# Attention and a low-rank mixer with its two layers on one core: batch 0 mixed by channel blocks, early layer products, w1's first half loaded ahead of batch 1, and batch 1's pairs moved into the later batches' loop

## The chip, the cores and the metric

The kernel runs on one core of one Trainium2 chip. The metric is the device time of one execution in microseconds (us); the median of three runs before the change is 366.27 us (366.23 to 368.55).

## The reference

There are 8 batches, 8 heads, 576 tokens of 64 channels, and 16 "beacon" keys and values ahead of each head's own. The attention is causal, except that all queries see the beacons. Its output, heads side by side, is x (576 tokens by 512 channels); a low-rank mix over tokens and a two-layer network follow.

```python
scores = scale * np.matmul(q, k_all.transpose(0, 1, 3, 2))      # k_all: beacon_k, then k
scores = np.where(causal, -1000000000.0, scores)
a = np.exp(scores - scores.max(-1, keepdims=True))
a /= a.sum(-1, keepdims=True) + 1e-09
x = np.matmul(a, v_all)                                         # heads put side by side
xt = x.transpose(0, 2, 1)
h = xt @ U @ V                                                  # U: 576 x 32, V: 32 x 576
u = x + h.transpose(0, 2, 1)
ch = np.maximum(u @ w_ch1, 0.0) @ w_ch2                         # 512 -> 2048 -> 512
return u + ch
```

## The kernel before

The order of every engine's instructions is the order in which the program writes them. Five engines work side by side: PE (TensorE, matrix products), DVE (VectorE), ACT (ScalarE), POOL (GpSimd, which here issues the casting loads and does a few casts) and SP (which issues the loads of batch 0's q and k, the DMA transposes and the stores).

**Pairs.** Two heads are one pair; a batch has four pairs (NH2 = 4), and pairs are counted through the batches: 0 to 3 are batch 0, 4 to 7 batch 1. For each pair there are these units:

- Regrouping (`regroup`, L220): q and k of the pair are copied into token order (`pr`).
- `qkT_units` (L223): five PE transposes each of q and k into PSUM (`tps`, L229, L231), then two DVE copies each into `qT` and `kT` (L232, L233). From pair 12 on DMA transposes and `order_units` (L257) do this instead.
- `score_units` (L267): `sc[0]` has the scores of key groups 0 and 1 (L286) and four exps on ACT (L292), `sc[1]` groups 2 and 3 and four more exps, `sc[2]` the causal masks on DVE (L273, L275). `sc[0](n)` puts n identity matmuls ahead of the scores (`keep_warm`, L211).
- `av_unit` (L306), one per head: 15 products of exps with values (L310), reciprocal and multiply on DVE (L318, L319) into the batch's `xb`.

**Mix.** `mix_units` (L323) of a batch has `head` (L334: U's products for the four blocks of 128 channels, side by side on PE into one PSUM tile, copied to `qts`) and two `part`s (L348: token tiles 0 and 1, then 2 to 4; for each channel block the transpose of `xb`, L354, plus V's product, L364, copied into `uT` by ACT or DVE).

**Layers.** The mixed tokens of all batches stand in `uT`, cut into nine blocks of 512. `mlp_units` (L378) of a block has 16 `g_unit`s (first layer, four products of 512 columns and a relu on ACT or DVE, L397 to L403) and 16 quarter `c_unit`s (second layer, four products each; the last quarter also stores, L413 to L431). They go into `queue`; `fill(n)` issues the next n of them between the attention's units.

**The order.** Batches 0 and 1 (NF = 2) run in a first loop (L644). Its turn for pair p does the second scores of pair p + 1, the masks of p, the regrouping, transposes and copies of p + 2 around the two heads of p, and the first scores of p + 2. `FIRST` says how many units of the queue are spread over a turn: none in batch 0, then 10, 5, 4, 4. After a batch's last pair, `mix(b)` puts its mix into the queue; batch 0's comes out at once, as the queue is empty, and `feed` adds the layer units of the block that is complete. Batches 2 to 7 run in a second loop (L682), whose turn for pair p has another order: 

```python
seq = sc[0:1] + av[0:1] + qk[0:1] + sc[1:3] + qk[1:2] + av[1:2]
```

Here `sc` are the scores of p + 1, `qk` the transposes of p + 2, and regrouping stands ahead of all. `QUOTA` units of the queue go into a turn: 4 in batch 2, 9 after it. Between the loops, `fill(AHEAD)` issues 16 units.

**Loads.** POOL's queue has, in order: v of batch 0 in two halves, k and q of batch 1 in two halves (`HALVES`: heads 0 to 3, 4 to 7), the first half of its v, the two halves of w1 (`emit_w1`), the casts of U and V (`cast_small`), v's second half, w2 in two halves, and the loads of batch 2 (`load_batch`).

**Memory.** All PSUM tiles share eight banks (`pst`); the four exp tiles `expt0` to `expt3` are used by two pairs in turn.

Of the kernel before, what the change touches and what calls it, by code (L numbers as in the profile page):

```python
# [9 lines left out]
F16 = mybir.dt.float16  # L10
F32 = mybir.dt.float32
# [6 lines left out]
P = 128  # L18
# [9 lines left out]
def kernel(  # L28
# [13 lines left out]
    nc = tc.nc  # L42
# [17 lines left out]
    NT = NC  # L60
# [38 lines left out]
    def pst(shape, dtype, name):  # L99
        return psum.tile(shape, dtype, tag="ps", name=name)  # L100
# [61 lines left out]
    def beacon_load(eng, src, dst, hs):  # L162
        eng.dma_start(out=dst[0:Nb], in_=src[hs].rearrange("h p d -> p h d"))  # L163
# [24 lines left out]
    def k_loads(b, L, hs):  # L188
        main_load(nc.gpsimd, k[b], L[1][0][:, hs, :], hs)
        head_load(nc.gpsimd, k[b], L[0][0][:, hs, :], hs, Nb)  # L190
# [29 lines left out]
        copy(out=t, in_=by_token(L[1][i][:, 2 * c : 2 * c + 2, :]))  # L220
        return t

    def qkT_units(L, pr, qT, kT, c):  # L223

        hs = ds(2 * c, 2)

        def one(i, dst, w):
            ps = pst([P, SK], F16, name="tps")
            nc.tensor.transpose(ps[:, 0:NL], L[0][i][:NL, hs, :], ident[:NL, :NL])  # L229
            for j in range(4):  # L230
                nc.tensor.transpose(ps[:, ds(NL + P * j, P)], pr[i][:, j, :, :], ident)  # L231
            nc.vector.tensor_copy(out=dst[:, c, 0 : w - 4 * P], in_=ps[:, 0 : w - 4 * P])  # L232
            nc.vector.tensor_copy(  # L233
                out=dst[:, c, w - 4 * P : w].rearrange("x (p j) -> x p j", j=4),
                in_=ps[:, NL:SK].rearrange("x (j p) -> x p j", j=4),
            )

        return [lambda: one(1, qT, S), lambda: one(0, kT, SK)]
# [136 lines left out]

        return turn, head, [lambda: part([0, 1]), lambda: part([2, 3, 4])]

    def mlp_units(t0, n, dst, flip, turned=True):  # L378


        units = []
        gT = {}

        def turn():
            ut = utp.tile([P, 4, DM], F16, name="ut", tag="ut")
            for cc in range(NCC):
                nc.sync.dma_start_transpose(out=ut[:, :, ts(cc, P)], in_=uT[:, cc, ds(t0, 4 * P)])
            gT["u"] = ut

        def g_unit(dc):  # L390
            if dc == 0:
                gT["t"] = gtp.tile([P, NDC, 512], F16, name="gT", tag="gT")
                if turned:
                    turn()
            g = pst([P, 512], F32, name="gps")
            for cc in range(NCC):
                nc.tensor.matmul(  # L397
                    g[:, 0:n], w1[:, cc, ts(dc, P)], uT[:, cc, ds(t0, n)], start=(cc == 0), stop=(cc == NCC - 1)
                )
            if (dc % 3 if not turned else (dc + flip) % 2 or dc in (5, 6, 7)):  # L400
                nc.scalar.activation(out=gT["t"][:, dc, 0:n], in_=g[:, 0:n], func=AF.Relu)  # L401
            else:
                nc.vector.tensor_scalar_max(out=gT["t"][:, dc, 0:n], in0=g[:, 0:n], scalar1=0.0)  # L403

        cps = {}

        def c_unit(i, part):
            m = min(P, n - P * i)
            if part == 0:
                cps["t"] = pst([P, DM], F32, name="cps")  # L410
            ps = cps["t"]
            for dc in range(4 * part, 4 * part + 4):
                nc.tensor.matmul(  # L413
                    ps[:m, :], gT["t"][:, dc, ds(P * i, m)], w2[:, dc, :], start=(dc == 0),
                    stop=turned and dc == NDC - 1, skip_group_check=True,
                )
            if part == 3:
                ob = outp.tile([P, DM], F32, name="ob", tag="ob")
                if not turned:
                    for cc in range(NCC):  # L420
                        nc.tensor.matmul(
                            ps[:m, ts(cc, P)], uT[:, cc, ds(t0 + P * i, m)], ident, start=False, stop=True,
                            skip_group_check=True,
                        )
                if turned:
                    nc.vector.tensor_tensor(out=ob[:m, :], in0=ps[:m, :], in1=gT["u"][:m, i, :], op=ALU.add)  # L426
                elif i % 2:
                    nc.scalar.activation(out=ob[:m, :], in_=ps[:m, :], func=AF.Copy)
                else:
                    nc.vector.tensor_copy(out=ob[:m, :], in_=ps[:m, :])  # L430
                nc.sync.dma_start(out=dst(i, m), in_=ob[:m, :])  # L431

        units += [lambda dc=dc: g_unit(dc) for dc in range(NDC)]
        for i in range((n + P - 1) // P):
            units += [lambda i=i, part=part: c_unit(i, part) for part in range(4)]
        return units
# [29 lines left out]
    def load_batch(b):  # L466
        Ls[b] = qk_tiles()
        emit_loads(b, Ls[b], vss[b % 2])
# [35 lines left out]
    def group_first(c, i, copy):  # L504

        prs.setdefault(c, []).append(regroup(Ls[0], c, i, copy))
        hs = SETS[c]
        copy(out=Ls[0][0][i][:NL, hs, :], in_=raw["head"][:NL, i, hs, :])
# [28 lines left out]
    def qkT_of(p):  # L537
        b, c = divmod(p, NH2)
        new_qT_of(p)
        if p in raw_of:  # L540
            return order_units(raw_of[p], qTs[b], kTs[b % 2], c)
        return qkT_units(Ls[b], prs[p], qTs[b], kTs[b % 2], c)

    def scores_of(p):
        b, c = divmod(p, NH2)
# [9 lines left out]


    NF = 2
    HB = 3
    AHEAD = 16
    LAG = 12  # L560
    HINT = 5

    FIRST = [0, 0, 0, 0, 10, 5, 4, 4]

    QUOTA = {2: 4}

    IDLE = [10, 3, 2, 2]
    queue = []
# [9 lines left out]
    def feed(b):  # L578

        while state["t"] < NBLK and 512 * (state["t"] + 1) <= S * (b + 1):  # L580
            t = state["t"]
            queue.extend(
                mlp_units(512 * t, 512, lambda i, m, t=t: rows[ds(512 * t + P * i, m), :], t % 2, t > 0)
            )
            state["t"] += 1

    def mix(b):

        turned = b >= NF and len(queue) >= LAG + 5
        turn, head, parts = mix_units(xbs[b], S * b, turned)  # L590
        if turned:
            turn()
        n = LAG if turned else 2 if b >= NF else 0
        seq = queue[0:n] + [head] + queue[n : n + 3]
        rest = queue[n + 3 :]
        for u in parts:
            seq += [u] + rest[0:3]
            rest = rest[3:]
        queue[:] = seq + rest
        feed(b)  # L600

    with tc.manual_schedule(engines={ENG.PE, ENG.Activation, ENG.DVE, ENG.SP, ENG.Pool}):
# [25 lines left out]

        Ls[1] = qk_tiles()
        group_first(3, 0, G)  # L630
        k_loads(1, Ls[1], HALVES[0])
        q_loads(1, Ls[1], HALVES[0])
        beacon_load(nc.gpsimd, beacon_k[1], Ls[1][0][0], ALLH)
        k_loads(1, Ls[1], HALVES[1])
        q_loads(1, Ls[1], HALVES[1])
        v_loads(v[1], beacon_v[1], vss[1], HALVES[0])
        emit_w1(0)
        emit_w1(1)
        cast_small()
        v_loads(v[1], beacon_v[1], vss[1], HALVES[1])  # L640
        emit_w2()

        NP1 = NF * NH2
        for p in range(NP1):  # L644
            b, c = divmod(p, NH2)
            if c == 0 and NF <= b + 1:
                load_batch(b + 1)
            seq = [masks]
            if p + 1 < NP1:
                seq.insert(0, sc[1])  # L650
                masks = sc[2]
            av, qk, sc = av_of(p), [], []
            if p + 2 < NP1:
                if p == 0:
                    seq.append(lambda: group_first(2, 1, V))
                elif p > 1:
                    seq.append(lambda p=p: regroup_of(p + 2))
                qk = [lambda i=i, p=p: qkT_of(p + 2)[i]() for i in range(2)]
            seq += av[0:1] + qk + av[1:2]
            if p + 2 < NP1:  # L660
                new_qT_of(p + 2)
                sc = scores_of(p + 2)
                if p == 0:
                    seq.append(lambda: group_first(3, 1, act_copy))
                seq.append(lambda sc=sc, p=p: sc[0](IDLE[3] if p < NH2 else 0))
            done = 0
            for i, u in enumerate(seq):
                u()
                want = FIRST[p] * (i + 1) // len(seq)
                fill(want - done)  # L670
                done = want
            if c == NH2 - 1:
                mix(b)

        fill(AHEAD)
        regroup_of(NP1)
# [140 lines left out]
```

## Time and profile before

| | |
|---|---|
| median of three runs | 366.27 us (366.23 to 368.55) |
| the profiled execution | 367.15 us, span 365.5 us |
| PE busy | 349.8 us, 96% of the span |
| DVE, ACT, POOL busy | 204.7, 173.7 and 83.9 us |
| first layer (L397), second layer (L413) | 576 matmuls each, 135.7 and 134.4 us |
| exps (L292) | 256, 111.1 us, 531 ns each |
| DMA | 40.52 MB, mean 111 GB/s |

The page divides the span into 40 slices of 9.1 us, and each digit is the busy share of an engine in tenths. Matmuls overlap, so the mean of one (379 ns for 512 columns) is longer than the distance from one to the next. A line of the timeline gives start and duration in us, engine, line, operation, tiles and count, and in brackets the idle time ahead of it with what ended it.

### The profile page before, as it was taken

The page shows a single profiled execution, that of the slowest core. Times are in us where ns is not written, and L with a number is a line of the kernel's source. Part 1 is how long each engine was busy: PE and PEld are TensorE (multiplying, and loading weights), DVE is VectorE, ACT ScalarE, POOL GpSimd, SP SyncE. Part 2 cuts the span into 40 slices and gives each one's busy share as a digit, 9 for nine tenths or more (in the row PEclk, how much of TensorE's full clock was granted, in tenths as well). Part 3 has the DMA queues.
Part 4 walks back from the last instruction along what each step waited for, and adds up shares of the span by engine and source line. Part 5 has one row for each costly group of instructions (what it writes and reads, how often), then busy time and mean ns, then how long its engine had stood idle before and what let it go on. Part 6 is the DMA issues. An engine that isn't in the chain of part 4 may idle for free.

```text
span 365.5 us, 7721 instructions
## 1 busy us (share of the span) xinstructions
PE 349.8 (96%) x3040; PEld 173.5 (47%) x3040; DVE 204.7 (56%) x565; ACT 173.7 (48%) x382; POOL 83.9 (23%) x123
## 2 busy tenths in 40 slices
PE   7777999999999999999999999999999999999995
PEld 3544545545545444544445444544454555444442
DVE  4887664357776675565666666756566446223311
ACT  3976660177654553466436643674356503401300
POOL 8976436400336001800081005000000000000000
PEclk9989999999999999999999999999999999999999
DMA  9999999990999952999299917942141013013112
GB/s 178 212 151 184 194 201 156 176 170 10 145 136 163 178 80 59 121 190 137 60 111 206 131 35 101 150 74 41 63 120 26 2 57 103 14 59 87 31 44 79
DMA packets 117916, 40.52 MB, mean 111 GB/s; under 512 B 93680, under 2 KB 112112, under 8 KB 117872
## 3 DMA queue, kind: packets, MB, share of 16 engines
q0 software_dynamic: 65904, 17.54, 54.4%
q1 hardware_dynamic: 51520, 22.12, 31.0%
q8 instruction: 25, 0.41, 0.5%
q10 hardware_dynamic: 448, 0.30, 0.3%
q14 instruction: 19, 0.16, 0.1%
HBM read 37.86 MB, written 9.44 MB: 129 GB/s over the span
## 4 chain that ended last, share of the span: by engine, by line
PE 85%; DMA 6%; DVE 3%; ACT 2%; POOL 2%; issue 0%; DVEq 0%; POOLq 0%
PE cps L413 34%; PE gps L397 33%; PE po L310 6%; PE sps L286 6%; DMA w<-in_moe_w_ch_dram 2%; DMA raw<-pr 2%; PE ups L354 2%; DMA st<-in_q_dram 2%; ACT expt L292 2%; PE idle L211 1%; POOL vs L173 1%; DVE gT L403 1%; PE ups L364 1%; PE qtp L339 1%; PE tps L231 1%; DVE expt L273 1%
## 5 line engine op out<-in xcount | busy, mean ns | idle before, releaser
L292 ACT ACTIVATE expt<-sps 128x496 f16<-128x496 f32 (+2 forms) x256 | 111.1, 531 | 61.9 <-PE sps L286 61.7
L397 PE MATMUL gps<-uT,w 128*128 128x512 f16 x576 | 135.7, 379 | 1.8 <-ACT uT L374 1.2
L413 PE MATMUL cps<-w,gT 128*128 128x512 f16 x576 | 134.4, 379 | 0.0
L401 ACT ACTIVATE gT<-gps 128x512 f16<-128x512 f32 x86 | 51.8, 608 | 64.3 <-PE gps L397 62.0
L413 PEld LDWEIGHTS <-gT 128*128 128x128 f16 x576 | 52.3, 98 | 61.1 <-issue 3.7
L397 PEld LDWEIGHTS <-w 128*128 128x128 f16 x576 | 51.8, 98 | 60.8 <-issue 6.1
L403 DVE TENSOR_SCALAR gT<-gps 128x512 f16<-128x512 f32 x58 | 40.1, 691 | 45.7 <-PE gps L397 44.0
L426 DVE TENSOR_TENSOR ob<-cps,ut 128x512 f32<-128x512 f32 x32 | 22.1, 691 | 49.6 <-PE cps L413 49.1
L173 POOL DMA_DIRECT2D vs<-in_v_dram x50 | 40.8, 831 | 14.3 <-DMA st<-in_q_dram 4.9
L310 PEld LDWEIGHTS <-expt 128*128 128x128 f16 (+1 forms) x960 | 36.9, 98 | 15.0 <-DVE expt L273 2.2
L310 PE MATMUL po<-vs,expt 128*128 128x65 f16 (+1 forms) x960 | 40.3, 195 | 1.0 <-DVE expt L273 0.5
L286 PE MATMUL sps<-qT,kT 64*128 64x80 f16 (+4 forms) x384 | 33.4, 286 | 4.0 <-DVE kT L233 3.4
L319 DVE TENSOR_TENSOR xb<-po,rec 128x320 f16<-128x320 f32 x64 | 31.4, 491 | 2.2
L374 ACT ACTIVATE uT<-ups 128x240 f16<-128x240 f32 (+1 forms) x32 | 11.5, 416 | 39.3 <-PE ups L364 39.2
L273 DVE TENSOR_TENSOR expt<-expt,bigmask 128x512 f16<-128x512 f16 x64 | 26.7, 418 | 6.0 <-ACT expt L292 5.9
L163 POOL DMA_DIRECT2D vs<-in_beacon_v_dram x10 | 5.4, 538 | 100.6 <-PE po L310 100.3
L318 DVE RECIPROCAL rec<-po 128x5 f32<-128x5 f32 x64 | 12.0, 187 | 27.0 <-PE po L310 26.2
L286 PEld LDWEIGHTS <-kT 64*128 64x128 f16 x384 | 12.3, 95 | 30.1 <-issue 10.8
L372 DVE CAST uT<-ups 128x240 f16<-128x240 f32 (+1 forms) x32 | 13.1, 450 | 8.5 <-PE ups L364 8.5
L220 DVE COPY pr<-st 128x512 f16<-128x512 f16 x56 | 14.2, 296 | 1.0 <-DMA st<-in_q_dram 0.6
L260 DVE COPY qT<-raw 128x512 f16<-128x512 f16 x20 | 12.4, 619 | 2.7 <-DMA raw<-pr 2.7
L275 DVE TENSOR_TENSOR expt<-expt,mask 80x80 f16<-80x80 f16 x64 | 12.5, 196 | 0.0
(65 smaller groups left out, 157.2 us busy)
## 6 DMA issues: line engine op xcount, KB each, us to landing
out_dram<-ob SPq DMA_DIRECT2D x36, 256.0 KB, 2.3
w<-in_moe_w_ch_dram POOLq DMA_DIRECT2D x4, 1024.0 KB, 11.5
st<-in_k_dram POOLq DMA_DIRECT2D x6, 512.0 KB, 10.0
st<-in_q_dram POOLq DMA_DIRECT2D x6, 512.0 KB, 13.4
vs<-in_v_dram POOLq DMA_DIRECT2D x18, 128.0 KB, 7.5
stm<-in_k_dram SPq DMA_DIRECT2D x4, 256.0 KB, 4.6
vs<-in_v_dram POOLq DMA_DIRECT2D x12, 64.0 KB, 6.2
stm<-in_q_dram SPq DMA_DIRECT2D x3, 256.0 KB, 5.7
```

The lines of the kernel that those rows point to most:

```text
L173: nc.gpsimd.dma_start(out=dst[a : a + nq[j], j, :, :], in_=src[hs, ds(q0[j], nq[j]), :].rearrange("h p d -> p h d"))
L220: copy(out=t, in_=by_token(L[1][i][:, 2 * c : 2 * c + 2, :]))
L273: nc.vector.tensor_tensor(out=e4, in0=e4, in1=bigmask, op=ALU.min)
L286: nc.tensor.matmul(ps[g, i][:, ds(o, w)], kT[hp, c, ds(P * ch, P)], qT[hp, c, ds(qa, w)], start=True, stop=True,)
L292: nc.scalar.activation(out=ex[i][:, ds(SLOT * g, gw[g])], in_=ps[g, i][:, 0 : gw[g]], func=AF.Exp, scale=scale)
L310: nc.tensor.matmul(po[:, j, :], ex[0 : nk[c], ds(blk[(c, j)], P)], vs[0 : nk[c], ds(c * H * E + h * E, E)], start=(c == 0), stop=(c == j),)
L319: nc.vector.tensor_tensor(out=xb[:, :, ds(h * D, D)], in0=po[:, :, 0:D], in1=r.broadcast_to([P, NT, D]), op=ALU.mult)
L397: nc.tensor.matmul(g[:, 0:n], w1[:, cc, ts(dc, P)], uT[:, cc, ds(t0, n)], start=(cc == 0), stop=(cc == NCC - 1))
L401: nc.scalar.activation(out=gT["t"][:, dc, 0:n], in_=g[:, 0:n], func=AF.Relu)
L403: nc.vector.tensor_scalar_max(out=gT["t"][:, dc, 0:n], in0=g[:, 0:n], scalar1=0.0)
L413: nc.tensor.matmul(ps[:m, :], gT["t"][:, dc, ds(P * i, m)], w2[:, dc, :], start=(dc == 0), stop=turned and dc == NDC - 1, skip_group_check ...
L426: nc.vector.tensor_tensor(out=ob[:m, :], in0=ps[:m, :], in1=gT["u"][:m, i, :], op=ALU.add)
```

## The change

- The k copies of pair 0 are done by ACT instead of DVE (`copies`).
- POOL issues the first half of w1 ahead of k and q of batch 1, the casts of U and V and w1's second half behind the first halves of these.
- Batch 0 has a loop of its own (turns p = 0 to 3). Its mix goes by channel blocks (`mix_blocks`): U's products for blocks 0 and 1 as soon as pairs 0 and 1 are done, then these two blocks, then block 2 around the masks of pair 3, and block 3 after pair 3.
- The first four `g_unit`s of block 0 (`EARLY`) are split: the products of channel blocks 0 to 2 come ahead of batch 1's first transposes, the product of block 3 between the units of pair 4.
- Batch 1's pairs are no longer begun during batch 0. Pair 4's transposes and scores and pair 5's transposes follow the mix, and pairs 4 to 7 run in the second loop's order, each pair's regrouping directly ahead of its transposes, with 3, 2, 2 and 1 units of the queue per turn (`FIRST`).
- `AHEAD` is 8 instead of 16, `QUOTA` in batch 2 is 6 instead of 4, and batch 1's mix starts two units later in the queue.

```diff
-    def qkT_units(L, pr, qT, kT, c):
+    def qkT_units(L, pr, qT, kT, c, copies=(None, None)):
...
+            copy = copies[i] or nc.vector.tensor_copy
...
-            nc.vector.tensor_copy(out=dst[:, c, 0 : w - 4 * P], in_=ps[:, 0 : w - 4 * P])
-            nc.vector.tensor_copy(
+            copy(out=dst[:, c, 0 : w - 4 * P], in_=ps[:, 0 : w - 4 * P])
+            copy(
...
+    def mix_blocks(xb, u0):
+        qts = small.tile([P, P], F16, name="qts", tag="qts")
+
+        def head(ccs):
+            qtp = pst([P, P], F32, name="qtp")
+            for j in range(NT):
+                for cc in ccs:
+                    nc.tensor.matmul(
+                        qtp[ds(R * cc, R), :], Usb[: nq[j], j, :], xb[: nq[j], j, ts(cc, P)],
+                        start=(j == 0), stop=(j == NT - 1), skip_group_check=True,
+                        tile_position=(0, R * cc),
+                    )
+            rs = ds(R * ccs[0], R * len(ccs))
+            nc.vector.tensor_copy(out=qts[rs, :], in_=qtp[rs, :])
+
+        def block(cc, copies):
+            rs = ds(R * cc, R)
+            for js, copy in zip(([0, 1], [2, 3, 4]), copies):
+                a, n = q0[js[0]], sum(nq[j] for j in js)
+                ups = pst([P, n], F32, name="ups")
+                for j in js:
+                    nc.tensor.matmul(
+                        ups[:, ds(q0[j] - a, nq[j])], xb[: nq[j], j, ts(cc, P)], ident[: nq[j], : nq[j]],
+                        start=j == js[0], stop=False, skip_group_check=True,
+                    )
+                nc.tensor.matmul(
+                    ups, qts[rs, :], Vsb[rs, ds(a, n)], start=False, stop=True, skip_group_check=True,
+                )
+                copy(out=uT[:, cc, ds(u0 + a, n)], in_=ups)
...
-    def mlp_units(t0, n, dst, flip, turned=True):
+    def mlp_units(t0, n, dst, flip, turned=True, early=0):
...
-        def g_unit(dc):
+        def g_unit(dc, ccs=range(NCC)):
...
-            for cc in range(NCC):
+            for cc in ccs:
...
+            if ccs[-1] < NCC - 1:
+                return
...
-        units += [lambda dc=dc: g_unit(dc) for dc in range(NDC)]
+        for ccs in (range(NCC - 1), range(NCC - 1, NCC)):
+            units += [lambda dc=dc, ccs=ccs: g_unit(dc, ccs) for dc in range(early)]
+        units += [lambda dc=dc: g_unit(dc) for dc in range(early, NDC)]
...
-        return qkT_units(Ls[b], prs[p], qTs[b], kTs[b % 2], c)
+        return qkT_units(Ls[b], prs[p], qTs[b], kTs[b % 2], c, (act_copy, None) if p == 0 else (None, None))
...
+    NP1 = NF * NH2
...
-    AHEAD = 16
+    AHEAD = 8
...
-    FIRST = [0, 0, 0, 0, 10, 5, 4, 4]
-
-    QUOTA = {2: 4}
+    EARLY = 4
+    FIRST = [3, 2, 2, 1]
+
+    QUOTA = {2: 6}
...
-        n = LAG if turned else 2 if b >= NF else 0
+        n = LAG if turned else 2
...
+        emit_w1(0)
         k_loads(1, Ls[1], HALVES[0])
         q_loads(1, Ls[1], HALVES[0])
         beacon_load(nc.gpsimd, beacon_k[1], Ls[1][0][0], ALLH)
+        cast_small()
+        emit_w1(1)
+        v_loads(v[1], beacon_v[1], vss[1], HALVES[0])
         k_loads(1, Ls[1], HALVES[1])
         q_loads(1, Ls[1], HALVES[1])
-        v_loads(v[1], beacon_v[1], vss[1], HALVES[0])
-        emit_w1(0)
-        emit_w1(1)
-        cast_small()
         v_loads(v[1], beacon_v[1], vss[1], HALVES[1])
         emit_w2()
...
+        for p in range(NH2):
+            if p < NH2 - 1:
+                sc[1]()
+            if p < NH2 - 1:
+                masks()
+            av = av_of(p)
+            if p < 2:
                 masks = sc[2]
+                if p == 0:
+                    group_first(2, 1, V)
+                run(av[0:1] + turned_of(p + 2) + av[1:2], 0)
+                if p == 0:
+                    group_first(3, 1, act_copy)
+                sc = scores_of(p + 2)
+                sc[0](IDLE[3])
+            else:
+                masks = sc[2]
+                run(av, 0)
+            if p == NH2 - 2:
+                head, block = mix_blocks(xbs[0], 0)
+                head([0, 1])
+                for cc, copies in ((0, (act_copy, act_copy)), (1, (act_copy, act_copy))):
+                    block(cc, copies)
+                head([2])
+                masks()
+                block(2, (V, V))
+        feed(0)
+        load_batch(2)
+        fill(EARLY // 2)
+        head([NCC - 1])
+        block(NCC - 1, (V, act_copy))
+        fill(EARLY // 2)
+        regroup_of(4)
+        run(turned_of(4), 1)
+        sc = scores_of(4)
+        run(sc[0:2], 1)
+        regroup_of(5)
+        run(turned_of(5), 1)
+        run(sc[2:3], 2)
+        for p in range(NH2, NP1):
+            sc = scores_of(p + 1) if p + 1 < NP1 else []
+            qk = []
             if p + 2 < NP1:
+                qk = turned_of(p + 2)
+                qk[0] = lambda p=p, u=qk[0]: (regroup_of(p + 2), u())
+            av = av_of(p)
+            seq = sc[0:1] + av[0:1] + qk[0:1] + sc[1:3] + qk[1:2] + av[1:2]
             done = 0
             for i, u in enumerate(seq):
                 u()
-                want = FIRST[p] * (i + 1) // len(seq)
+                want = FIRST[p - NH2] * (i + 1) // len(seq)
                 fill(want - done)
                 done = want
-            if c == NH2 - 1:
-                mix(b)
+        mix(1)
```

(`run(us, n)` issues the units `us` with `fill(n)` behind each; `turned_of(p)` are the two transposing units of pair p. The old body of the first loop, which the new loops replace, is left out of this diff.)

More of the change, by code (lines that the diff above doesn't have):

```diff
@@ L376, in mix_units @@
         return turn, head, [lambda: part([0, 1]), lambda: part([2, 3, 4])]
-    def mlp_units(t0, n, dst, flip, turned=True):
+    def mix_blocks(xb, u0):
[25 more added lines that the diff above has]
+                copy(out=uT[:, cc, ds(u0 + a, n)], in_=ups)
+        return head, block
+    def mlp_units(t0, n, dst, flip, turned=True, early=0):
         units = []
         gT = {}
+        gps = {}
         def turn():
@@ L388, in turn @@
             gT["u"] = ut
-        def g_unit(dc):
-            if dc == 0:
+        def g_unit(dc, ccs=range(NCC)):
+            if dc == 0 and ccs[0] == 0:
                 gT["t"] = gtp.tile([P, NDC, 512], F16, name="gT", tag="gT")
@@ L394, in g_unit @@
                     turn()
-            g = pst([P, 512], F32, name="gps")
-            for cc in range(NCC):
+            if ccs[0] == 0:
+                gps[dc] = pst([P, 512], F32, name="gps")
+            g = gps[dc]
+            for cc in ccs:
                 nc.tensor.matmul(
@@ L582, in feed @@
             queue.extend(
-                mlp_units(512 * t, 512, lambda i, m, t=t: rows[ds(512 * t + P * i, m), :], t % 2, t > 0)
+                mlp_units(
+                    512 * t, 512, lambda i, m, t=t: rows[ds(512 * t + P * i, m), :], t % 2, t > 0, 0 if t else EARLY
+                )
             )
@@ L633 @@
         beacon_load(nc.gpsimd, beacon_k[1], Ls[1][0][0], ALLH)
+        cast_small()
+        emit_w1(1)
+        v_loads(v[1], beacon_v[1], vss[1], HALVES[0])
         k_loads(1, Ls[1], HALVES[1])
         q_loads(1, Ls[1], HALVES[1])
-        v_loads(v[1], beacon_v[1], vss[1], HALVES[0])
-        emit_w1(0)
-        emit_w1(1)
-        cast_small()
         v_loads(v[1], beacon_v[1], vss[1], HALVES[1])
         emit_w2()
[L643 to L650, printed above, removed]
-                masks = sc[2]
-            av, qk, sc = av_of(p), [], []
-            if p + 2 < NP1:
[L654 to L665, printed above, removed]
@@ new lines, in run, with turned_of @@
+        def run(us, n):
+            for u in us:
+                u()
+                fill(n)
+        def turned_of(p):
+            return [lambda i=i: qkT_of(p)[i]() for i in range(2)]
+        for p in range(NH2):
[5 more added lines that the diff above has]
+            if p < 2:
+                masks = sc[2]
+                if p == 0:
[16 more added lines that the diff above has]
+                block(2, (V, V))
```

## The prediction

> **What bounds the kernel now.** I read the busy slices of the page first, then stretches of 5 us, then TensorE's timeline where it is not full.
>
> ```profile
> span 365.5 us, 7721 instructions
> PE   7777999999999999999999999999999999999995
> PEclk9989999999999999999999999999999999999999
> ```
>
> TensorE is full from the fifth slice on; only the first four (36 us) and the last one have room. So whatever the change does, it can win only in the first 36 us, and it loses wherever it makes a new hole behind them.
>
> ```profile
> 20.00:25.00 5.00, 3.27 (x52) 2.11 (x50) 3.94 (x14) 3.22 (x8) 3.54 (x6) 0.85 1.54 164
> 25.00:30.00 5.00, 4.21 (x64) 2.73 (x62) 4.25 (x15) 3.60 (x9) 5.00 (x11) 0.81 1.22 107
> 30.00:35.00 5.00, 3.69 (x72) 2.56 (x69) 3.41 (x13) 4.49 (x12) 2.88 (x5) 1.00 1.12 211
> 35.00:40.00 5.00, 5.00 (x44) 2.79 (x45) 3.52 (x9) 1.19 (x2) 0.90 (x1) 1.00 1.40 195
> ```
>
> The columns are the stretch, its length, then busy us of PE, its weight loads, DVE, ACT and POOL, the granted clock, DMA share and GB/s. From 20 to 35 us PE is busy 11.2 of 15 us and part of that runs at a lower clock; from 35 us on it has no hole. What ends the holes:
>
> ```profile
> 20.47 0.61 PE L310 MATMUL po<-vs,expt 128*128 128x65 f16 x15 [0.17 <-DVE expt L275]
> 22.65 0.21 PE L229 MATMUL tps<-ident,hd 80*128 80x80 f16 x1 [1.56 <-DMA hd<-in_q_dram]
> 26.25 0.92 PE L310 MATMUL po<-vs,expt 128*128 128x65 f16 x15
> 34.93 1.90 PE L397 MATMUL gps<-uT,w 128*128 128x512 f16 x8 [0.58 <-DMA w<-in_moe_w_ch_dram]
> ```
>
> Batch 1's first pair waits 1.56 us for its load, and the first layer product starts at 34.93, when w1's first half lands. (At 26.25 one head's values product takes 0.92 instead of about 0.61: the clock is half there.) The fourth view is the loop into which batch 1's pairs are moved, as batch 2 runs it now:
>
> ```profile
> 82.86 0.58 PE L286 MATMUL sps<-qT,kT 64*128 64x496 f16 x4
> 83.36 1.95 ACT L292 ACTIVATE expt<-sps 128x496 f16<-128x496 f32 x4
> 85.16 0.64 ACT L401 ACTIVATE gT<-gps 128x512 f16<-128x512 f32 x1
> 85.64 1.59 ACT L292 ACTIVATE expt<-sps 128x496 f16<-128x496 f32 x4
> 87.15 0.42 DVE L273 TENSOR_TENSOR expt<-expt,bigmask 128x512 f16<-128x512 f16 x1
> 88.04 0.19 DVE L232 COPY kT<-tps 128x80 f16<-128x80 f16 x1
> 88.15 0.68 DVE L233 COPY kT<-tps 128x512 f16<-128x512 f16 x1
> 88.90 0.58 PE L286 MATMUL sps<-qT,kT 64*128 64x496 f16 x4
> ```
>
> This is a closed ring: scores of a pair, four exps, a relu, four exps, masks, the k copies of the pair after it, its scores. It takes 88.90 - 82.86 = 6.04 us (0.50 to the first exp, 1.80, 0.48, 1.51, 0.89 for masks, 0.86 for k copies and the way to PE), and about 5.6 without the relu. TensorE's work in it is a pair's 2.35 us (transposes 0.54, scores 0.90, two heads at 0.46) and four layer units at 0.865, 5.8 in all, so the ring is hidden with 0.2 us to spare. With fewer units it is not.
>
> **The change, part by part.** *k copies of pair 0 to ACT.* DVE now copies q from 6.57 and k until 8.06, scores start at 8.12. An ACT copy of 512 columns took 0.60 (L374's rows 0.42 for 240 to 336); the two beside DVE's end near 7.6. Pair 1 still waits for its load at 8.56, and ACT then runs 16 exps without a hole; by the mask of pair 0, which waits for ACT, about 0.4 us reaches pair 3 (bounds 0 and 0.5). I take 0.4.
>
> *Warm-ups.* Four of 23 identity matmuls go. They stand in PE's waits: nothing; if the clock falls for it, see the second rival.
>
> *Loads.* POOL issues w1's first half (0.78 us) at about 14.1, where k of batch 1 went. The transfers behind each other on that queue keep their order: in the trace q's first half landed at 22.33 (15.49 + 6.84) and w1's halves came at about 5.3 us each. So w1's first half lands near 24.5, q's first half near 22.3 + 5.3 = 27.6, the second halves of k and q (now near 25.7) behind both halves of w1 and half of v (3.5): 25.7 + 10.6 + 3.5 = 39.8.
>
> ```profile
> 26.16 1.52 POOL L149 DMA_DIRECT2D w<-in_moe_w_ch_dram x2
> 35.17 0.90 POOL L155 DMA_DIRECT2D w<-in_moe_w_ch_dram x1 [2.29 <-DMA w<-in_moe_w_ch_dram]
> 41.81 0.88 POOL L155 DMA_DIRECT2D w<-in_moe_w_ch_dram x1 [5.74 <-issue]
> ```
>
> POOL holds an issue until the one eight before it has landed (w2's halves stand exactly eight behind w1's). By that, k's second half is held until w1's second lands (near 33), behind it v's second half and w2; the queue is still full then, so it costs nothing. The small casts now wait for V (issued by 14.4, 5.7 to land: 20.1) and hold the second half of w1 until 20.8, while 6 us of transfers lie ahead of it: nothing. w2 is done near 52.5, as before, and is wanted near 58.
>
> *Batch 0's mix by blocks.* The same matmuls, but U's products no longer go four side by side: 15 steps for 5 at 0.055, and V's eight one after another (0.10 and 0.14) for two groups of 0.2: about 1.1 us more PE, in a stretch where PE waits for exps and masks anyway.
>
> *From 20 to 32 us*, on three engines: the scores of pair 3 stand at 19.0, its exps end at 22.8 (eight at 0.42). Heads 4 and 5: 20.1 to 21.0. Then reciprocal and multiply (0.62 a head) on DVE, the copy qts at 22.2, blocks 0 and 1 until 23.2, block 2's head, masks until 24.8, heads 6 and 7 24.45 to 25.4, two early products (three quarters of 0.865) until 26.7, a wait of 0.35 for head 7, block 3 until 28.2, two more until 29.5. Batch 1's first pair is transposed there, both w1's half and q having landed; DVE does q copies 0.7, a relu 0.6, k copies 0.7 before its scores can start at 32.05, and PE idles 1.5 of it. By 37.96 pair 4's scores, pair 5's transposes and eight layer units are done. That is 0.54 + 0.90 + 0.54 + 8 x 0.865 = 8.9 us of work; before has by then both pairs' transposes and scores, head 8, half of pair 6's transposes and three units, 6.2: 2.7 us in hand.
>
> *Batch 1 in the ring.* Its units per pair are 3, 2, 2, 1 (FIRST), so PE has 4.95, 4.1 and 3.5 us for a ring of 5.6 to 6.04. In the first two rounds regrouping moved between the reciprocal and the transpose: after a head ends, 0.2 + 0.62 + 0.40 + 0.1 = 1.3 us pass before PE can go on, and the second scores stand behind it (in the fourth view they start 2.2 after the first, here 3.4). Round one: scores at 37.96, exps to 40.5, second scores 41.4, relu, exps to 43.6, masks 44.5, a relu 45.1, k copies 45.85: 7.9 us. Round two: from 45.9, second scores 48.5, exps 50.4, masks 51.3, k 52.05: 6.2. Round three has no k copies, but heads 14 and 15 wait for exps until 55.9 and the mask until 56.4; they end at 57.4, unit 15 at 58.2.
>
> *The sum.* At 58.2 all 16 second-layer units of block 0 are left. Before has 14 left at 58.03, so it stood there at 58.03 - 2 x 0.865 = 56.3. The change is 1.9 late. Six units for four in batch 2 give 7.5 us of PE work for its ring of 6.04, so two of its holes close, 0.18 at 82 and 0.68 at 101 (times between matmul starts above the usual 0.216); the one at 76 (0.57) returns, as regrouping 0.8 stands behind the mix's copies: 0.9 back. The 62 units for 55 by batch 2's end shift work to the tail, which is full PE either way. Together +1.0 us: the profiled execution's 367.15 (span 365.5 and 1.65 around it) becomes 368.15; it lies 0.9 over the median, so on the median's scale 366.27 + 1.0 = **367.3**.
>
> **Rivals.** *Faster: the ring hides.* If second scores, exps and masks overlap as well as a full PE would let them, 37.96 to the end of unit 15 is work alone, 14.4 us (three pairs' scores, eight heads, two pairs' transposes, eight units): 52.4, 3.9 ahead of 56.3; with the 0.9 that is -4.8, 361.5. For it: 2.7 us in hand at 38. Against it: the ring row, which no PE order shortens; half of the gain is likelier (364).
>
> *Slower: the clock falls in batch 1.* The half clock of 23.5 to 26.9 followed a hole of 1.56 us with little else in its 3.4 us. My schedule has 1.2 us of matmuls from 44.0 to 47.4. If the clock then halves for 3.4 us, 2.6 us of work take up to 5.2, less 0.8 of waits: +1 to +2.6. [...] With second halves of k and q 1 to 2 us late (39.8 wanted at 39.8; everything on PE behind them waits) it gives +3 to +5.6: 369.3 to 371.9.
> [...]
>
> *Nothing moves.* The products only trade places and each hole filled opens one of equal size: 366.3.
>
> **How the numbers follow.** Forecast (0 to +2.6 us, its own range 366.3 to 368.9): 0.45; nothing to a gain under 2 us: 0.12; the ring partly or wholly hidden: 0.17; the clock or late loads: 0.26. Range: 363.4 (a half gain and some) to 370.4 (the slower rival's middle). One per cent, 3.7 us, is about what a measurement of this kernel can tell from no change. Over it: the upper half of the hidden ring, 0.11 faster; about half of the slower rival, 0.14 slower; the rest, 0.75, within.
>
> **What would show it.** Right: the first layer product near 25.5, a hole near 31, scores of pairs 5, 6 and 7 starting 6 to 8 us apart with PE idle 1 to 2 us before each, head 15 ending near 57, batch 2 without holes. Wrong: those scores 5 us apart (faster rival), or PEclk below 9 beyond slice four, or transposes of pair 6 waiting for hd or st (slower).

## The result, and the profile after

The changed kernel takes 372.51 us (median of four runs, 371.29 to 374.14); the kernel before, beside it on the same chip, 366.25 us (366.07 to 368.55). The ratio is 1.0161, with a 95% interval of 1.0135 to 1.0187: slower by 1.6%, where 367.3 was forecast and 363.4 to 370.4 allowed. (Here and below a ratio is estimated from the fast executions alone, so it need not equal the ratio of the two medians.) The profiled execution takes 371.29 us, its span is 369.6.

The page of the changed kernel, its first line and the busy slices:

```profile
span 369.6 us, 7703 instructions
PE   7786879999999999999999999999999999999995
PEclk9999899999999999999999999999999999999999
```

The third slice (18 to 28 us) is fuller than it was, but the fourth, fifth and sixth (28 to 55 us) are down to 6, 8 and 7, where they were 7, 9 and 9, and the clock dips in the fifth. The same stretches of 5 us as before the change (stretch, length, busy us of PE, weight loads, DVE, ACT, POOL, then clock, DMA share, GB/s):

```profile
20.00:25.00 5.00, 4.29 (x67) 2.70 (x61) 2.76 (x10) 4.60 (x12) 2.31 (x4) 1.00 1.32 200
25.00:30.00 5.00, 4.67 (x54) 2.63 (x55) 3.95 (x15) 0.10 (x1) 4.20 (x6) 1.00 1.25 208
30.00:35.00 5.00, 3.51 (x30) 1.64 (x29) 2.34 (x7) 1.82 (x4) 1.84 (x3) 1.00 1.58 147
35.00:40.00 5.00, 3.41 (x18) 1.74 (x17) 2.19 (x5) 3.37 (x9) 5.00 (x8) 0.73 1.44 115
```

From 20 to 30 us PE is fuller, as was meant: 8.96 us busy instead of 7.48. From 30 to 40 us it is busy for 6.92 instead of 8.69, and part of that runs at a low clock. TensorE's timeline shows where:

```profile
22.68 0.27 PE L406 MATMUL ups<-Vsb,qts 32*128 32x240 f16 x1 [0.51 <-DVE qts L394]
22.89 0.32 PE L402 MATMUL ups<-ident,xb 128*128 128x128 f16 x3
...
25.85 1.09 PE L311 MATMUL po<-vs,expt 128*128 128x65 f16 x30
26.78 1.46 PE L435 MATMUL gps<-uT,w 128*128 128x512 f16 x6
...
33.72 0.58 PE L287 MATMUL sps<-qT,kT 64*128 64x496 f16 x4 [1.49 <-DVE kT L234]
...
37.28 0.61 PE L232 MATMUL tps<-ident,pr 128*128 128x128 f16 x4 [1.39 <-DVE pr L220]
37.68 1.91 PE L435 MATMUL gps<-uT,w 128*128 128x512 f16 x4
...
42.96 0.58 PE L287 MATMUL sps<-qT,kT 64*128 64x496 f16 x4
...
45.38 0.40 PE L232 MATMUL tps<-ident,pr 128*128 128x128 f16 x4 [1.24 <-DVE pr L220]
...
50.62 0.58 PE L287 MATMUL sps<-qT,kT 64*128 64x496 f16 x4 [1.01 <-DVE kT L234]
...
52.98 0.40 PE L232 MATMUL tps<-ident,pr 128*128 128x128 f16 x4 [1.18 <-DVE pr L220]
...
56.65 0.58 PE L287 MATMUL sps<-qT,kT 64*128 64x496 f16 x4 [0.31 <-DVE kT L234]
```

Three waits of 1.39, 1.24 and 1.18 us are for `pr`, the regrouping of pairs 5, 6 and 7 on DVE. After the first of them four layer products take from 37.68 to 39.39, 0.43 each instead of 0.216: the granted clock is 0.5 there. What held the regrouping of pair 5 is in DVE's timeline:

```profile
35.82 0.69 DVE L443 TENSOR_SCALAR gT<-gps 128x512 f16<-128x512 f32 x1 [2.16 <-PE gps L435]
36.43 0.80 DVE L220 COPY pr<-st 128x512 f16<-128x512 f16 x2
```

DVE was idle for 2.16 us, in front of a relu that waited for PE; the regrouping stands behind that relu in program order, and the relu's product stands on PE behind the second scores of pair 4, which wait for exps. No data held the copies: their order did, as the second experiment shows.

### The profile page after: what moved, and what is told of

Read it like the earlier page. It is cut to its first block, busy times and chain, and to the rows that moved or that the text cites. A ratio compares the mean times of both kernels' runs of the same rounds, so it can differ in the third digit from the quotient of the medians.

```text
span 369.6 us, 7703 instructions
## 1 busy us (share of the span) xinstructions
PE 352.4 (95%) x3036; PEld 173.7 (47%) x3036; DVE 206.2 (56%) x564; ACT 175.0 (47%) x385; POOL 84.2 (23%) x123
## 4 chain that ended last, share of the span: by engine, by line
PE 87%; DVE 6%; DMA 3%; ACT 2%; issue 1%; ACTq 0%
PE cps L453 34%; PE gps L435 32%; PE po L311 7%; PE sps L287 7%; PE ups L355 2%; ACT expt L293 2%; PE tps L232 1%; DMA sth<-in_q_dram 1%; DMA raw<-pr 1%; DMA stm<-in_q_dram 1%; PE ups L365 1%; DVE gT L443 1%; DVE kT L234 1%; DVE xb L320 1%; PE qtp L340 1%
## 5 line engine op out<-in xcount | busy, mean ns | idle before, releaser
L435 PE MATMUL gps<-uT,w 128*128 128x512 f16 x576 | 137.2, 382 | 0.0
L443 DVE TENSOR_SCALAR gT<-gps 128x512 f16<-128x512 f32 x58 | 40.0, 689 | 38.3 <-PE gps L435 37.2
L466 DVE TENSOR_TENSOR ob<-cps,ut 128x512 f32<-128x512 f32 x32 | 22.1, 691 | 50.9 <-PE cps L453 50.4
L375 ACT ACTIVATE uT<-ups 128x240 f16<-128x240 f32 (+1 forms) x28 | 10.0, 412 | 34.2 <-PE ups L365 34.2
L373 DVE CAST uT<-ups 128x240 f16<-128x240 f32 (+1 forms) x28 | 11.5, 451 | 6.2 <-PE ups L365 6.1
L232 PE MATMUL tps<-ident,pr 128*128 128x128 f16 x96 | 9.8, 231 | 4.0 <-DVE pr L220 4.0
```

The lines of the kernel that those rows point to most:

```text
L435: nc.tensor.matmul(g[:, 0:n], w1[:, cc, ts(dc, P)], uT[:, cc, ds(t0, n)], start=(cc == 0), stop=(cc == NCC - 1))
```

## The experiments

Two theories at first. R: the regrouping stands too late in DVE's order, so PE stops for it three times, and the first stop also brings on the half clock. C: the low clock of batch 1's thin stretches is the cost, and matmuls put into the holes would keep it up; the order matters little. Two lesser ones: too few layer units are issued in batch 1, and the block form of the mix costs PE time. An execution's time goes with its mean clock (spans of the kernel before: 365.5 us on average at 0.998 or more, 366.9 at 0.993 to 0.995; last section), so the ratios have wide intervals; kernels of one group ran on one chip. A stage of one program also starts up to 0.8 us earlier or later from trace to trace (pair 3's scores at 19.08 to 19.90), so a stage's length is read between two points of one trace.

**More matmuls in the holes.** Identity matmuls, as the kernel has them in batch 0, ahead of the waits of batch 1:

```diff
         sc = scores_of(4)
+        sc[0] = lambda u=sc[0]: u(5)
...
+        keep_warm(pst([P, 512], F32, name="idle"), 5)
         run(turned_of(5), 1)
...
+            if p > NH2 and sc:
+                sc[0] = lambda u=sc[0]: u(3)
...
-                qk[0] = lambda p=p, u=qk[0]: (regroup_of(p + 2), u())
+                qk[0] = lambda p=p, u=qk[0]: (regroup_of(p + 2), keep_warm(pst([P, 512], F32, name="idle"), 4), u())
```

> The changed kernel plus identity matmuls in the holes of batch 1 (5 ahead of pair 4's scores, 5 ahead of pair 5's transposes, 4 ahead of those of pairs 6 and 7, 3 ahead of the scores of pairs 6 and 7); they compute nothing that is used. Theory C (the clock: a thin window between 33.8 and 37.3 us lets the clock fall to half for 3.4 us, and executions differ by how many such windows they catch): no half clock between 20 and 62 us, the transposes of pair 5 and four layer units at 0.865 instead of 1.71 us, 371.3 becomes about 369.6 in the best execution, the median 372.5 falls by 2 to 3 us and the executions lie within 1 us. Rival R (the waits of the ring and of regrouping alone): the clock makes no odds behind waits, the median stays within 0.7 us of 372.5.

Measured: 373.45 us against 368.20, ratio 1.0119 (1.0072 to 1.0166): the loss stays, and a gain on the changed kernel (1.0161) can't be told. In the profiled execution (span 372.8) batch 1 kept its clock and took less time: from pair 4's scores to the end of the first-layer units 27.15 us (36.82 to 63.97) instead of 28.59. But batch 0, which the edit doesn't touch, lost its clock in three stretches, one from 11.7 to 15.1 us and these two:

```profile
22.00:25.40 3.40, 2.83 (x33) 1.59 (x31) 1.20 (x5) 3.15 (x9) 0.70 (x1) 1.00 1.54 192
25.40:28.80 3.40, 3.24 (x38) 2.21 (x37) 2.87 (x10) 0.01 (x1) 2.66 (x5) 0.50 1.18 212
28.80:32.20 3.40, 3.32 (x14) 1.19 (x12) 0.82 (x3) 0.00 (x0) 0.96 (x2) 0.50 1.72 175
```

Here the half clock follows a stretch in which PE was busy for 2.83 of 3.40 us, with the mix by blocks. So busy time on the page does not say where the clock falls. The clock of batch 1 is thus a part of the cost, but as a remedy the extra matmuls failed.

**All three regroupings earlier.** Pair 5's directly behind pair 4's, those of pairs 6 and 7 at the start of the turn:

```diff
         regroup_of(4)
+        regroup_of(5)
         run(turned_of(4), 1)
...
-        regroup_of(5)
         run(turned_of(5), 1)
...
+                regroup_of(p + 2)
                 qk = turned_of(p + 2)
-                qk[0] = lambda p=p, u=qk[0]: (regroup_of(p + 2), u())
```

> The changed kernel with regrouping ahead: pair 5's right behind pair 4's, those of pairs 6 and 7 at the start of the turn, as in batch 2. Theory R: the three waits of transposes for DVE (1.39, 1.24 and 1.18 us) go; scores of pairs 5 to 6 come 6.0 instead of 7.7 us apart, 6 to 7 stay at 6.0; the hole of 1.39 was also the one that let the clock fall, so about 1.4 + 1.7 + 1.6 = 4.7 us less, 366.6 to 368. Rival C alone: only what the clock took, 1.5 to 2.5 us less. Rival D (the second halves of k and q land too late for it, and DVE waits for them with masks and copies queued behind): no gain or a loss.

Measured: 368.09 us against 368.20, ratio 1.0003 (0.9958 to 1.0047); the profiled span is 364.9, at a mean clock of 1.0. The loss against the kernel before is gone, with one edit of order on DVE. Scores of pairs 4 to 7 in PE's timeline:

```profile
33.42 0.58 PE L287 MATMUL sps<-qT,kT 64*128 64x496 f16 x4 [1.49 <-DVE kT L234]
...
39.65 0.58 PE L287 MATMUL sps<-qT,kT 64*128 64x496 f16 x4
...
46.05 0.58 PE L287 MATMUL sps<-qT,kT 64*128 64x496 f16 x4 [1.16 <-DVE kT L234]
...
51.18 0.58 PE L287 MATMUL sps<-qT,kT 64*128 64x496 f16 x4 [0.54 <-DVE kT L234]
```

Pair 5's copies now run right behind pair 4's, long before the relu at 35.52, so their data were there. In DVE's timeline (four copies, two for each pair):

```profile
29.43 0.89 DVE L220 COPY pr<-st 128x512 f16<-128x512 f16 x4
```

No wait for `pr` is left in batch 1. Pair 5's scores come 6.23 us after pair 4's instead of 9.24; the last first-layer unit of the block ends at 56.84 instead of 62.31. R is shown.

**More layer units in batch 1**, alone and with the earlier regrouping:

```diff
-    FIRST = [3, 2, 2, 1]
+    FIRST = [5, 4, 4, 3]
```

> The changed kernel with 5, 4, 4, 3 layer units in the turns of batch 1 instead of 3, 2, 2, 1. Theory R: the ring of 5.6 to 7.7 us stays, but 8 more units (6.9 us) stand in its holes (1.24 + 1.01 + 1.18 + 0.31 us shown as waits, 4 to 5 us in all): 3 to 4 us less, 368.5 to 369.5, the clock's window at 37.3 stays as it comes before. Rival: units ahead of the second scores push exps and masks back by as much, ring 1 us longer a round: less than 1.5 us of gain.

> Both of the last two: regrouping ahead, and 5, 4, 4, 3 units. Theory R: the holes of batch 1 close but for the one ahead of pair 4's scores (1.5 us); what is lost behind 34 us is under 2 us, and 365 to 366.5 result, level with the kernel before or 1 us better. Rival (what batch 0's waits no longer cover is lost for good): no better than 368.

Measured: 377.89 us, ratio 1.0296 (1.0220 to 1.0372), and 374.57 us, ratio 1.0196 (1.0122 to 1.0269). In both a gain was expected and a loss came. The page of the second shows where to look:

```profile
PE   7787999989999999999999999999999997999995
```

Near 305 us there is a new gap. What PE waited for from 200 us on (engine, tile and line that waited, the one waited for, total us, times, longest):

```profile
PE ups L365 <- DVE qts L346: 2.9, 2, 2.7
```

The kernel with the earlier regrouping alone has no wait in that list. Eight units more are issued in batch 1 (16 for 8), 8 x 0.865 = 6.9 us of PE work, and the later turns take as many as ever; so, it is argued, the queue runs short, and PE has nothing left to do while it waits for a mix. The profiled span is 7.4 us longer (372.3 against 364.9). From 60 us on PE waits 7.1 us in this trace and 0.9 with the earlier regrouping alone. 6.5 of the 7.1 stand in or behind the mixes of the batches, on their `qts` and `uT` copies, from 75 us on; half clock follows the longest of these waits (2.7 us; the clock is 0.83 from 310 to 320 us, and 0.995 over the span against 1.0).

**Parts of the change alone**, on a second chip (before: 368.01 us): the k copies of pair 0 on ACT, put into the kernel before; `AHEAD` 8 and `QUOTA` 6, put into the kernel before; the changed kernel with the old order of loads; and the changed kernel with batch 0's mix in one piece behind pair 3.

```diff
...
-        return qkT_units(Ls[b], prs[p], qTs[b], kTs[b % 2], c)
+        return qkT_units(Ls[b], prs[p], qTs[b], kTs[b % 2], c, (act_copy, None) if p == 0 else (None, None))
```

> The kernel before with one part of the change alone: the k copies of pair 0 on ACT. My step: 0.4 us earlier at pair 3 and so at the end, 365.9. Rival, from the trace of the changed kernel, where pair 1's scores start at 11.45 (before 11.41) and pair 3's at 19.27 (before 19.42): 0.15 us at most, not to be told from nothing.

```diff
-    AHEAD = 16
+    AHEAD = 8
...
-    QUOTA = {2: 4}
+    QUOTA = {2: 6}
```

> The kernel before with another part alone: 6 units per turn in batch 2 instead of 4 and 8 instead of 16 between the loops. My step: the holes at 82 and 101 us (0.18 and 0.68) go, 0.9 us less, 365.4. The changed kernel's trace gave 1.9 back behind 62 us, so by that 364.4. Rival: the gain hangs on where the queue stands when batch 2 begins, and here it begins 8 units earlier: no change.

```diff
-        emit_w1(0)
         k_loads(1, Ls[1], HALVES[0])
...
-        cast_small()
-        emit_w1(1)
-        v_loads(v[1], beacon_v[1], vss[1], HALVES[0])
         k_loads(1, Ls[1], HALVES[1])
         q_loads(1, Ls[1], HALVES[1])
+        cast_small()
+        v_loads(v[1], beacon_v[1], vss[1], HALVES[0])
+        emit_w1(0)
+        emit_w1(1)
```

> The changed kernel with the first halves and second halves of k and q of batch 1 ahead of w1 again (the casts of U and V stay early, behind k and q). If the early products are what the early w1 serves: w1's first half lands near 34 instead of 25, the first product waits from 26.8 to 34 and all behind it with it, 5 to 7 us more than the changed kernel: 377 to 379. Rival: batch 1's pairs wait less for loads and half of it comes back: 374 to 375.

```diff
             if p == NH2 - 2:
-                head, block = mix_blocks(xbs[0], 0)
-                head([0, 1])
...
                 masks()
-                block(2, (V, V))
+        _, head, parts = mix_units(xbs[0], 0, False)
+        head()
+        for u in parts:
+            u()
         feed(0)
         load_batch(2)
-        fill(EARLY // 2)
-        head([NCC - 1])
-        block(NCC - 1, (V, act_copy))
-        fill(EARLY // 2)
+        fill(EARLY)
```

> The changed kernel with batch 0's mix in one piece behind pair 3, four blocks side by side as before, instead of block by block; the four early products follow it. By blocks the mix took PE about 4.0 us of its own (21.5 to 25.85 and 28.25 to 29.8, less waits), whole about 2.2. Theory B (the block form costs PE more than it hides): equal or up to 1 us faster, 371.5 to 372.5. Rival (the block form hides the mix behind pair 3's exps, as it is meant to): the whole mix stands open behind pair 3, 2 to 3 us slower, 374.5 to 375.5.

| | median us | ratio to before | profiled span us |
|---|---|---|---|
| k copies on ACT | 367.85 | 0.9978 (0.9935 to 1.0021) | 367.4 |
| `AHEAD` 8, `QUOTA` 6 | 366.76 | 0.9943 (0.9895 to 0.9991) | 364.5 |
| old order of loads | 381.18 | 1.0361 (1.0285 to 1.0437) | 377.4 |
| mix in one piece | 371.54 | 1.0103 (1.0029 to 1.0178) | 369.5 |

The copies on ACT can't be told from nothing. `AHEAD` and `QUOTA` alone make the kernel before a little faster, by 0.6%; it is the only one of the versions here that can be told from it as faster, and only just. Its profiled execution has a mean clock of 0.995, that of the kernel before 0.994, and its span is 1.0 us shorter (364.5 against 365.5). The earlier load of w1 is needed for the rest of the change: without it the time is longer than the 377 to 379 expected, as the first layer product waits, in PE's timeline:

```profile
35.00 2.74 PE L435 MATMUL gps<-uT,w 128*128 128x512 f16 x6 [7.74 <-DMA w<-in_moe_w_ch_dram]
```

The mix by blocks gains nothing: in one piece, pair 4's scores start 13.66 us after pair 3's (19.68 to 33.34) instead of 14.45 (19.27 to 33.72); the spans are 369.5 and 369.6. In one piece PE waits 1.48 us for exps, 0.65 for `xb` and 0.53 for the mix's copies. By blocks these waits are filled, but by longer work of the mix itself.

**Which regrouping, and a best version**, on a third chip (before: 367.75 us): pair 5's regrouping alone moved (the first two hunks of the earlier regrouping), those of pairs 6 and 7 alone (its last hunk), the changed kernel once more, and all three moved together with pair 4's k copies on ACT and both its transposes ahead of two layer units:

```diff
-... (act_copy, None) if p == 0 else (None, None))
+... (act_copy, None) if p in (0, NH2) else (None, None))
...
+        regroup_of(5)
-        run(turned_of(4), 1)
+        run(turned_of(4), 0)
+        fill(2)
```

> The changed kernel with one regrouping moved: pair 5's right behind pair 4's, ahead of the relu of unit 3. Theory R with the clock: the hole of 1.39 us at 35.7 goes, the window 33.8 to 37.3 is then over 2 us busy and keeps its clock (1.7 us), the turns of pairs 6 and 7 stay as they are: about 3 us less than the changed kernel in executions of equal clock, span near 366.6. If the turns are what counts: 1 us less at most.

> The changed kernel with the other two regroupings moved: those of pairs 6 and 7 to the start of their turns. Theory R: the holes of 1.24 and 1.18 us go and the rounds become about 5 to 5.5 us as in the kernel with all three moved (there 40.2 to 46.05 to 51.18), 1.5 to 2 us less than the changed kernel, span near 367.8; the clock still falls near 37 us.

> The changed kernel again, on this chip beside the others. Span 369.6 at a mean clock of 0.994, and 1.5 to 2 us more for each further window of half clock (0.005 of the mean); no execution at a mean clock of 1.0, as the hole at 35.7 always leaves one window thin.

> All three regroupings moved, and for pair 4 the k copies on ACT beside DVE's q copies, with both transposes ahead of the last quarters of units 0 and 1: the hole ahead of pair 4's scores falls from 1.49 to about 0.5 us. 1 us less than the kernel with the three regroupings moved, span near 363.9 at full clock, and ahead of the kernel before by 0.3 to 0.6%. Rival: the ring behind it takes the 1 us up again and nothing is gained.

| | median us | ratio to before | profiled span us |
|---|---|---|---|
| pair 5 only | 371.26 | 1.0105 (1.0024 to 1.0185) | 369.2 |
| pairs 6 and 7 only | 372.65 | 1.0111 (1.0011 to 1.0211) | 372.9 |
| changed kernel | 374.47 | 1.0209 (1.0113 to 1.0305) | 370.3 |
| all three, and pair 4's copies on ACT | 366.75 | 0.9981 (0.9940 to 1.0022) | 364.4 |

The medians fall by 3.2 and 1.8 us for the two halves, but the intervals overlap; only both together are told from the changed kernel. The changed kernel came out as expected again: no execution kept its full clock (means of 0.975 to 0.993). The spans of this table hold different numbers of low-clock stretches (five in that of pairs 6 and 7, whose mean clock is 0.977). Within the traces both halves show: with pair 5's regrouping moved, its scores come 6.24 us after pair 4's instead of 9.24; with those of pairs 6 and 7 moved, pair 5's scores to the end of the first-layer units take 17.18 us instead of 19.35. With pair 5 alone the span falls less than was expected (369.2, expected 366.6), as the half clock is not gone, it has moved:

```profile
47.50:50.90 3.40, 1.38 (x24) 0.86 (x24) 2.46 (x9) 2.42 (x5) 0.83 (x1) 1.00 1.23 204
50.90:54.30 3.40, 3.40 (x28) 1.81 (x26) 1.99 (x8) 2.13 (x5) 0.00 (x0) 0.51 1.30 203
```

The thin stretch is now between the scores of pairs 5 and 6, where the regrouping of pair 7 and k of pair 6 are waited for. In the last version the hole ahead of pair 4's scores is 0.39 us instead of 1.49, and that is kept: from pair 3's scores to pair 4's it takes 13.23 us instead of 14.34, and from there to the end of the first-layer units 23.42 in both. That this end is only 0.36 earlier than with the three regroupings alone (56.48 against 56.84) comes from pair 3, which started 0.75 later in this execution. By its ratio it still can't be told from the kernel before, nor from the earlier regrouping alone, so the version with the lowest ratio stays `AHEAD` and `QUOTA` alone.

## Why the prediction was wrong, step by step

- *k copies of pair 0 to ACT: 0.4 us reaches pair 3.* Not seen. Pair 0's scores start at 7.71 instead of 8.12, but with `AHEAD` and `QUOTA` alone, where DVE still does these copies, they start at 7.72 too. Pair 3's start at 19.42 and 19.36 in these two traces without the copies on ACT, and at 19.08 to 19.90 in the nine traces with them that kept their clock until then. A gain of 0.4 there is not borne out, and no smaller one can be told.
- *Loads.* Right. The first product waits for no load, and POOL held k's second half as worked out, until 33.16 (forecast 33), at no cost:

```profile
33.16 0.61 POOL L160 DMA_DIRECT2D hd<-in_k_dram  x1 [3.22 <-DMA w<-in_moe_w_ch_dram]
```

- *The mix by blocks: 1.1 us more PE, in a stretch where PE waits anyway.* Mis-sized, and the cover was not there. Each V product with 32 rows takes 0.21 or 0.25 us to the next start (22.68 to 22.89) instead of 0.10 or 0.14, and from 22.7 on PE's own work set the end (0.17 us of waits until heads 6 and 7). These start at 25.85 (forecast 24.45), the first layer product at 26.78 (about 25.4), pair 4's scores at 33.72 (32.05): 1.67 late, 0.27 of it at pair 3's scores already (19.27, forecast 19.0).
- *"By 37.96 pair 4's scores, pair 5's transposes and eight layer units are done."* This is the step that failed. It counted PE's work against PE's time and gave the regrouping of pair 5 no place in DVE's order and no time. In program order it stands behind the relu at 35.82. So pair 5's scores start at 42.96 where 37.96 was forecast, 5.0 late: 1.67 from above, 1.39 for the wait, about 1.7 for the half clock that followed it, and a rest of 0.24, most of it a wait for an exp (0.19). With this one regrouping moved, 3.0 us of it are gone (6.24 instead of 9.24 from pair 4's scores). The prediction had found the same wait for pairs 6 and 7, where it wrote out DVE's order; for pair 5 it did not.
- *The ring of batch 1.* Right in mechanism and size: the rounds take 50.62 - 42.96 = 7.66 us (forecast 7.9) and 6.03 (6.2), and the holes for regrouping are 1.24 and 1.18 (1.3). The faster rival, pairs 5 us apart, did not come.
- *The slower rival: the clock falls in batch 1.* It came as described, a thin window and then 3.4 us at half clock, but in another place: the thin window was 33.8 to 37.2, not 44.0 to 47.4. Its price was 1.7 us, within the 1 to 2.6 worked out. How thin a window must be for this no run shows: PE is busy for 1.90 us of this one, with a hole of 1.39, and for 1.91 of the one before it, with a hole of 1.49, and behind that one the clock stayed at 1.00. The window and its neighbours:

```profile
30.40:33.80 3.40, 1.91 (x19) 1.05 (x18) 2.09 (x5) 0.60 (x1) 0.64 (x2) 1.00 1.86 166
33.80:37.20 3.40, 1.90 (x15) 0.51 (x15) 1.38 (x3) 3.07 (x8) 3.40 (x6) 1.00 1.03 103
37.20:40.60 3.40, 3.32 (x15) 1.81 (x16) 1.28 (x5) 1.41 (x4) 3.40 (x5) 0.51 1.67 114
```

- *0.9 given back in batch 2.* Right for `AHEAD` and `QUOTA` by themselves: with them alone the holes at 82 and 101 us are gone and the profiled span is 1.0 shorter. Too little for the whole change. The last first-layer unit ends at 62.31, 6.0 later than the 56.3 worked out for before; the span is 4.1 longer, so 1.9 came back. Two holes that were not in the forecast are gone, both where a layer product waited for the mix's copies:

```profile
119.33 1.02 PE L397 MATMUL gps<-uT,w 128*128 128x512 f16 x4 [0.53 <-ACT uT L374]
...
158.11 1.89 PE L397 MATMUL gps<-uT,w 128*128 128x512 f16 x8 [0.67 <-ACT uT L374]
```

  These two lines are of PE's timeline of the kernel before. With `AHEAD` and `QUOTA` alone both remain (0.53 and 0.66); with the three regroupings moved both are gone as well. The number of units that batch 2 leaves behind, 62 instead of 55, fits this; it was not tried alone.
- *The sum.* Forecast: 1.9 late, 0.9 back, +1.0. Measured in the profiled executions: 1.9 + 5.0 for pair 5 - 0.9 for the turns after it (rounds 0.4 shorter than forecast, the last turn 0.5) = 6.0 late, 1.9 back, +4.1. The medians lie 6.3 apart. The two us between are a matter of which executions were profiled: that of the kernel before lies 0.9 over its median, that of the changed kernel 1.2 under its own. What goes with the spread is the clock: the eight executions of the changed kernel have mean clocks of 0.975 to 0.995 and none reaches 0.998, while 17 of 45 of the kernel before on the later three chips and 5 of 10 with the regrouping moved do.

## What to carry to other kernels

When a stage is moved, write out the order of the engine that prepares it, not only of the one that is full: here a copy whose data were there stood behind a relu that waited 2.16 us for the very engine that needed the copy. Move such preparations up in program order before filling the holes with other work; filler taken from a queue that later stages live on is missing there. And look at stretches in which the matrix engine is thin: here the clock was at half for 3.41 us behind some of them, at about 1.4 to 1.7 us each. A start time from one trace against that of another can mislead by as much as the effect; compare distances within each trace.

## What the runs showed of the hardware that was not expected

In the traces of the two kernels the granted clock falls from 1.0 to 0.5 in the middle of the run, once in each, and for 3.41 us: from 23.51 to 26.92 us before the change, from 37.25 to 40.67 after it. With the identity matmuls it is at 0.50 from 25.4 to 32.2, two such stretches, while PE is busy for 3.24 of the first 3.40 us. What PE did in the 3.4 us ahead of half clock in four traces, and in three stretches with full clock behind them:

| | stretch, us | PE busy, us | longest wait of PE, us | clock in the 3.4 us behind it |
|---|---|---|---|---|
| kernel before | 20.1 to 23.5 | 1.67 | 1.56 | 0.50 |
| changed kernel | 33.8 to 37.2 | 1.90 | 1.39 | 0.51 |
| pair 5's regrouping moved | 47.5 to 50.9 | 1.38 | 1.18 | 0.51 |
| identity matmuls | 22.0 to 25.4 | 2.83 | 0.57 | 0.50 |
| changed kernel | 30.4 to 33.8 | 1.91 | 1.49 | 1.00 |
| changed kernel | 20.2 to 23.6 | 2.77 | 0.51 | 1.00 |
| kernel before | 9.9 to 13.3 | 2.27 | 0.72 | 1.00 |

Neither column sorts them: 2.83 us of busy time has half clock behind it and 1.91 full clock, a wait of 0.57 us has half clock behind it and one of 1.49 full clock. What decides is not shown by these runs.

Half clock went with longer executions: of the kernel before on the later three chips, 17 executions at a mean clock of 0.998 or more have spans of 365.5 us on average, 19 at 0.993 to 0.995 have 366.9, and 6 at 0.989 to 0.991 have 368.7. One stretch of 3.41 us at half clock takes 0.005 off the mean over such a span, so by an estimate from these numbers one stretch made an execution about 1.4 us longer, and two about 3.2.
